# V computed once for each tile of 128 tokens and copied into its blocks; K's last four heads of chunks 2 and 3 computed in the padding of seven weight tiles; transfers issued from two queues

## The chip, the cores and the metric

The kernel runs on one core of a Trainium2 chip. The core has five engines, each with an instruction queue of its own that is worked off in order: TensorE (PE, matrix products into PSUM), VectorE (DVE), ScalarE (ACT), GpSimd (POOL) and SyncE (SP), which here only issues transfers (DMAs). Transfers can be issued by SP and by ACT; on ACT such an issue stands in the same queue as its arithmetic. The metric is the device time of one launch in microseconds (us); before the change the median of three runs is 171.44 us.

## What is computed

Inputs and output are bf16; 2048 tokens of width D = 448; 16 heads of Dh = 28; F = 1792. Cut to what matters:

```python
mod = silu(c) @ w_mod                      # six vectors: sa, ca, ga, sb, cb, gb
h = layernorm(x) * (1 + ca) + sa
q, k, v = split(h @ wqkv)                  # (16 heads, 2048, 28) each
idx = pos[:, None] - 2 * arange(8)         # each token sees itself and 7 earlier ones, 2 apart
logits = einsum(q, k[idx]) * 28 ** -0.5    # masked where idx < 0
o = einsum(softmax(logits), v[idx])
x = x + ga * (o @ wo)
h = layernorm(x) * (1 + cb) + sb
out = x + gb * (silu(h @ w1) @ w2)
```

## The kernel before

**Tokens.** Since a token sees only tokens of its own parity, the sequence is held as two parities of 1024 positions. It is worked in four chunks (`NC = 4`) of `CP = 256` positions of both parities, that is, 512 tokens. Attention works in nine blocks (`BLOCKS`, 0 to 8): block b has 112 queries of each parity (128 in block 0) and the 128 keys from position 112·b on, so neighbouring blocks share 16 keys.

**Stages of a chunk.** `norm1` normalises the 512 tokens and brings them, modulated, with the features on the partitions, into a buffer `h` (`h1_0`, `h1_1`, `wqk` in turn). For chunk 0 this is done in two halves with transposes on PE (L529) and the modulation on ACT and DVE (L536, L538); for the others by transposing DMAs on SP (L550) and a modulation in place (L555, L557). `project` computes Q and K by tiles of four heads, each head padded from 28 to 32 columns (weights `wp`, `wp3`, filled by four copies `pad`, L564 and L566): a "duo" is one tile of Q and the same tile of K, 14 matmuls (L627) of 64 contracted rows each, in pairs that run side by side, first seven "straight" then, after a `turn`, the "crossed" rest; a turn is an empty instruction of POOL (L312) that the crossed matmuls wait for. There are four duos a chunk (eight of half the width in chunk 0). The result is evicted to `qk` (L630). V is computed for each block (L638, 14 matmuls of 448 columns) and evicted into one of four buffers `v` (L642). Since a block's keys start up to 128 positions ahead of the chunk, `h` is 384 wide and a copy `halo` (L611) brings the end of the chunk before.

**Attention and the rest.** `logits` (L670) and the exponential (ACT, L678) run for each block and parity, DVE masks (L704), `values` multiplies with V (L730), DVE normalises (L735, L736), a transposing DMA (L740) brings the result to `oT`, `out_proj` (L753) and DVE (L768) add it to `x_all`. Then a second layernorm (`n2`), the first feed-forward product (L791, evicted with silu by ACT, L794), the second (L808; L832 for the last 256 tokens), the addition (L823, L838) and the store (L826, L841). `gate` (L450) and `mods` (L433) compute the modulation vectors from `w_mod`.

**What sets the order.** Every step is an operation of a `Plan`; the string `ORDER` lists all operations by number, and each engine's queue gets its steps in that order (a letter a or v puts a step on ACT or DVE). Buffers are handed out in the same order: four PSUM tiles `ps`, five `p`, four `v`. All DMAs share eight semaphores: a queue issues the ninth DMA only when an earlier one on the same semaphore has landed, and it holds everything behind it in that queue until then. Before the change nearly all DMAs are SP's; ACT issues three at the start (L368: the second half of chunk 0's `x` and the vector c).

The function is called twice: a second, `safe` version of the layer stands behind a flag worked out from the softmax sums and is skipped here.

Of the kernel before, what the change touches and what calls it, by code (L numbers as in the profile page):

```python
# [35 lines left out]
HW = 128 + CP  # L36
# [40 lines left out]
def half(j):  # L77
    return slice(K3 * j, K3 * j + K3)
# [33 lines left out]
def dram(ap, row, col, dims):  # L112

    w = ap.ap[0][0]
    return bass.AP(ap.tensor, ap.offset + row * w + col, [[r * w + c, n] for r, c, n in dims])


class Plan:

# [879 lines left out]
```

## Time and profile before

| what | value |
|---|---|
| median of three runs (lowest, highest) | 171.44 us (171.24, 171.64) |
| the profiled execution's own time | 171.64 us |
| its span, first to last instruction | 169.9 us |
| busy: PE, ACT, DVE, POOL | 162.0, 114.5, 96.1, 33.2 us |
| mean granted clock of PE | 0.989 |
| matmuls of V (L638), of Q and K (L627) | 126 and 280 |

The span and the time outside it (1.74 us) make the execution's own time. The profile has these views: busy time by engine; the chain of waits, followed back from the last instruction and shown in order of time (start, duration, what); groups of instructions by line; a timeline; sums by windows of time; who waited for whom; the transfers, with their time from issue to landing. A row of the timeline holds the start, the time that the row's instructions cover, the engine, line and operation, the tiles, the number of instructions (x14), and in brackets the engine's idle time before it with what ended it.

### The profile page before, as it was taken

How to read it: one execution, taken by the hardware profiler on the slowest of the kernel's cores; microseconds unless marked ns; L12 is line 12 of the kernel's file. 1: busy time of each engine (PE TensorE's matmuls, PEld its weight loads, DVE VectorE, ACT ScalarE, POOL GpSimd, SP SyncE). 2: the span in 40 equal slices, each digit the busy share in tenths (PEclk: the TensorE clock that was granted, in tenths of full speed). 3: DMA queues.
4: the chain of work that ended last, by engine and by line, in shares of the span. 5: the costliest groups of instructions: out<-in, count | busy, mean ns of one | idle time of the engine just before them, and what ended most of it. 6: DMA issues, size and time to landing. Idle time of an engine off the chain costs nothing.

```text
span 169.9 us, 4812 instructions
## 1 busy us (share of the span) xinstructions
PE 162.0 (95%) x2015; PEld 83.9 (49%) x2015; DVE 96.1 (57%) x189; ACT 114.5 (67%) x163; POOL 33.2 (20%) x88
## 2 busy tenths in 40 slices
PE   7799999899999999999999999999999999999990
PEld 2258644545554564455644544655544444445450
DVE  4777999899979963895352577732473000000451
ACT  3148999999876889999878998662767862420000
POOL 7342424730502221132000205120150000000000
PEclk9959999999999999999999999999999999999999
DMA  4994448489979874022020030086008000000031
GB/s 142 289 326 165 99 94 314 78 202 242 176 185 252 177 198 106 0 66 46 20 54 0 4 90 22 2 112 178 6 10 224 0 4 0 0 4 0 38 136 64
DMA packets 32054, 17.51 MB, mean 103 GB/s; under 512 B 23896, under 2 KB 31640, under 8 KB 32024
## 3 DMA queue, kind: packets, MB, share of 16 engines
q1 hardware_dynamic: 31872, 16.90, 39.9%
q8 instruction: 17, 0.28, 0.7%
q10 hardware_dynamic: 152, 0.23, 0.5%
q14 instruction: 13, 0.11, 0.2%
HBM read 9.12 MB, written 1.84 MB: 64 GB/s over the span
## 4 chain that ended last, share of the span: by engine, by line
PE 75%; ACT 10%; DMA 6%; issue 3%; DVE 2%; POOL 1%; ACTq 0%; POOLq 0%
PE ps L791 25%; PE ps L808 22%; PE ps L627 7%; PE ps L753 6%; PE ps L638 5%; ACT p L678 4%; PE ps L730 4%; DMA wqk<-in_A_wqkv_dram 3%; PE ps L832 3%; PE ps L670 3%; DMA x_all<-in_A_x_dram 2%; ACT h L536 2%; ACT qk L630 1%; POOL rs L487 1%; ACT both L480 1%
## 5 line engine op out<-in xcount | busy, mean ns | idle before, releaser
L791 PE MATMUL ps<-h,w 64*128 64x512 bf16 x392 | 44.7, 376 | 0.0
L808 PE MATMUL ps<-w,both 64*128 64x448 bf16 x392 | 39.9, 349 | 0.0
L794 ACT ACTIVATE both<-ps 128x1024 bf16<-128x1024 f32 x28 | 27.3, 1023 | 13.9 <-PE ps L791 13.8
L678 ACT ACTIVATE p<-ps 128x896 bf16<-128x896 f32 (+1 forms) x36 | 31.5, 928 | 3.3 <-PE ps L670 3.2
L791 PEld LDWEIGHTS <-w 64*128 64x128 bf16 x392 | 19.5, 94 | 21.6
L808 PEld LDWEIGHTS <-both 64*128 64x128 bf16 x392 | 18.9, 94 | 17.7
L823 DVE TENSOR_TENSOR ot<-ps,x_all 128x896 bf16<-128x896 f32 x7 | 7.6, 1088 | 34.6 <-PE ps L808 34.3
L627 PE MATMUL ps<-h,wp 64*128 64x256 bf16 (+1 forms) x224 | 20.4, 323 | 0.6 <-ACT h L536 0.4
L627 PEld LDWEIGHTS <-wp 64*128 64x128 bf16 x280 | 13.9, 94 | 11.3 <-issue 1.1
L704 DVE TENSOR_TENSOR p<-p,maskb 128x1792 bf16<-128x1792 bf16 (+1 forms) x18 | 19.3, 1098 | 0.0
L768 DVE SCALAR_TENSOR_TENSOR x_all<-ps,x_all 128x448 bf16<-128x448 f32 x16 | 9.3, 618 | 9.7 <-PE ps L753 9.7
L487 POOL TENSOR_TENSOR rs<-rs,negh 128x2 f32<-128x2 f32 x16 | 13.8, 861 | 1.3
L753 PE MATMUL ps<-wo,oT 64*128 64x448 bf16 x112 | 13.0, 350 | 0.0
L480 ACT ACTIVATE wqk<-x_all,mv 128x448 bf16<-128x448 bf16 x16 | 10.7, 667 | 3.2 <-POOL mv L477 3.0
L477 POOL TENSOR_SCALAR mv<-sums 128x2 f32<-128x2 f32 x10 | 4.8, 479 | 40.0 <-DVE x_all L768 22.2
L638 PE MATMUL ps<-wv,h 64*128 64x448 bf16 x98 | 11.3, 350 | 0.2
L557 DVE TENSOR_SCALAR h<-h,modc 128x512 bf16<-128x512 bf16 x19 | 6.8, 408 | 6.6 <-DMA h<-xn 6.6
L630 ACT CAST qk<-ps 128x1024 bf16<-128x1024 f32 (+1 forms) x12 | 10.0, 871 | 0.7 <-PE ps L627 0.7
L321 ACT ACT_TABLE_LOAD x8 | 10.3, 1283 | 0.1
L486 POOL TENSOR_SCALAR rs<-mv 128x2 f32<-128x2 f32 x10 | 3.6, 356 | 33.3 <-ACT wqk L480 14.5
L736 DVE TENSOR_TENSOR o<-ps,rc 112x896 bf16<-112x896 f32 (+1 forms) x9 | 9.8, 1091 | 0.4
L501 DVE TENSOR_SCALAR xn<-x_all,mv,rs 128x512 bf16<-128x512 bf16 x23 | 8.8, 406 | 1.7 <-POOL rs L487 1.7
(84 smaller groups left out, 161.8 us busy)
## 6 DMA issues: line engine op xcount, KB each, us to landing
out_dram<-ot SPq DMA_DIRECT2D x7, 224.0 KB, 2.2
both<-in_w_mod_dram SPq DMA_DIRECT2D x2, 672.0 KB, 6.0
x_all<-in_A_x_dram SPq DMA_DIRECT2D x3, 448.0 KB, 7.0
w<-in_B_w_dram SPq DMA_DIRECT2D x3, 448.0 KB, 4.2
w<-in_B_w_dram SPq DMA_DIRECT2D x1, 896.0 KB, 5.3
both<-in_w_mod_dram SPq DMA_DIRECT2D x2, 336.0 KB, 5.8
w<-in_B_w_dram SPq DMA_DIRECT2D x1, 672.0 KB, 5.4
wqk<-in_A_wqkv_dram SPq DMA_DIRECT2D x1, 448.0 KB, 5.7
```

The source lines that it names most:

```text
L321: P.load = lambda t: S.preload_act_table(ACTF.Exp if t == "e" else ACTF.Silu)
L480: S.activation(out=scratch[late], in_=x_all[:, us[j], :], func=ACTF.Square, bias=mv[:, j, 0:1], accum_out=mv[:, j, 1:2])
L487: G.tensor_tensor(out=rs[:, j:j + n], in0=rs[:, j:j + n], in1=negh[:, 0:n], op=ALU.pow)
L627: return T.matmul(ps[:, j, 0:2 * n], lhsT=w.rearrange("p h d -> p (h d)"), rhs=h[rows, :, t, c0:c0 + n], start=start, stop=stop)
L630: copy_on(o)(out=qk[:, :, g, :, s0:s0 + n], in_=ps[:, :, 0:2 * n].rearrange("p j (t s) -> p j t s", t=2))
L638: return T.matmul(ps[:, j, 0:D], lhsT=h[rows, j, t, b0:b0 + 128], rhs=wv[rows, t, :], start=start, stop=stop)
L678: S.activation(out=out_, in_=ps[:, :, 0:4 * nq].rearrange("p j (g q) -> p j g q", q=nq), func=ACTF.Exp, scale=SCALE)
L704: V.tensor_tensor(out=p, in0=p, in1=maskb[:, 1 if b == 0 else 0, 0:nq].unsqueeze(1).to_broadcast([128, H, nq]), op=ALU.mult)
L753: return T.matmul(box["ps"][:, j, 0:D], lhsT=oT[rows, j, kk, s0:s0 + 128], rhs=wo[rows, j, kk, :], start=start, stop=stop)
L791: return T.matmul(ps[:, j, :], lhsT=w, rhs=h[rows, :, t, :], start=start, stop=stop)
L794: S.activation(out=hid[:, k % 2, :, i, :], in_=ps[:], func=ACTF.Silu)
L808: return T.matmul(box["ps"][:, par, 0:D], lhsT=hid[rows, k % 2, f % 2, f // 2, 128 * (2 * i + par):128 * (2 * i + par) + 128], rhs=w2[rows ...
```

## The change

**V in tiles.** V is computed for eight tiles of 128 positions instead of nine blocks, each once, and evicted into three new buffers `va`. Blocks 0 and 8 read their tile directly. Each of the other seven blocks is put together from two neighbouring tiles by two transfers within SBUF (`vs`, 14 in all, 16 to 112 rows of 2048 bytes) into one of three buffers `v`. The `halo` copies go, and `h` is 256 wide.

**Q and K in seven tiles.** In chunks 2 and 3 K's last four heads (4 × 28 = 112 columns) are put into the padding columns of the seven other weight tiles (7 × 4 heads × 4 columns), by nine small copies on POOL (`fill`), two of which go into an extra weight tile `wq3`. The fourth duo then has a Q tile alone, with half the columns for each matmul (256 instead of 512). Four transfers a chunk (`mv`, 28 KB each) bring K's last heads from the padding rows to their place in `qk`. The projections of chunk 1 and later wait for the fills.

**Transfers.** A load, a `vs`, a `mv` or a store may stand on SP's queue or ACT's; `ORDER` says which. ACT now issues two loads of `w_mod` first, and 20 DMAs in all; the second half of chunk 0's `x` comes behind the weights of Q and K. Two pairs of loads of 64 rows (for `wqk3` and `w13`) become one load each, whose source is two pieces of 64 rows (`pairs_of`); a third load of this kind, of 28 KB, is new. `ORDER` is another string throughout, with another order of projections, of first-layer products and of table loads (6 in place of 8 behind the first).

```diff
-    NV, NP, NX, NO, NH, NB2 = (4, 5, 2, 2, 3, 2) if not safe else (3, 3, 2, 1, 3, 1)
+    NA, NV, NP, NX, NO, NH, NB2 = (3, 3, 5, 2, 2, 3, 2) if not safe else (3, 3, 3, 2, 1, 3, 1)
...
+def pairs_of(ap, r0, c0, r1, c1, n):
+
+    w = ap.ap[0][0]
+    return bass.AP(ap.tensor, ap.offset + r0 * w + c0, [[(r1 - r0) * w + c1 - c0, 2], [w, 64], [1, n]])
...
+    EITHER = ("sp", "act") if not safe else ("sp",)
+
+    def queue(o):
+        return nc.scalar if o["eng"] == "act" else nc.sync
...
-    ld_x = [[load(224, **first_x(0), run=1792, name="x0a"), load(224, **first_x(1), run=1792, q=nc.scalar, name="x0b")]]
+    ld_x = [[load(224, **first_x(0), run=1792, q=("sp",), name="x0a")]]
...
-    ld_ma = load_mod(0, 2 * D, [first])
+    ld_ma = load_mod(0, 2 * D, [], ("act",))
...
-    ld_qk = [[a], [b], [a], [load(56, wqk3[half(a), 0:D], A_wqkv[128 * (a + 1):128 * (a + 1) + K3, D * (1 - a):D * (2 - a)], late, name="wqk") for a in range(2)]]
+    ld_qk = [[a], [b], [a], [load(112, wqk3[:], pairs_of(A_wqkv, 128, D, 256, 0, D), late, name="wqk")]]
...
+    ld_x[0].append(load(224, after=[x["deps"][0] for x in [ld_qk[0][0], ld_qk[1][0], ld_qk[3][0]]], **first_x(1), run=1792, name="x0b"))
...
+    def fill(out_, m0, in_, t0, t1, deps, name="fill"):
+
+        to = out_[:, m0:m0 + 4 * (t1 - t0), DH:32].rearrange("p (t r) c -> p t r c", r=4)
+        return P.op(("pool", 300.0), lambda o: G.tensor_copy(out=to, in_=spread(in_, t0, t1)), deps, name=name)
...
-        halo[k] = P.op(either(60.0 + 0.83 * 8 * w, 60.0 + 0.26 * 8 * w), lambda o: copy_on(o)(out=h[:, :, :, 128 - w:128].rearrange("p t k s -> p (t k) s"),
...
+    def move(r, s0, n, deps):
+
+        return sp(680.0, lambda o: queue(o).dma_start(out=qk[32 * r:32 * r + DH, 1, 3, :, s0:s0 + n], in_=qk_t[32 * r + DH:32 * r + 32, 0:7, :, s0:s0 + n]), list(deps), 1700.0,
+                  kb=28.0, run=512, eng=EITHER, name="mv")[0]
...
-            for g in range(4):
+            for g in range(4 if k < 2 else 3):
...
+            if k > 1:
+
+                def make(ps, j, kk, rows, t, start, stop, c0=c0):
+                    w = wq3[rows, kk // 3] if j and kk in (1, 3) else wp[rows, kk, 12:16, :] if kk < 3 else wp3[rows, 12:16, :]
+                    return T.matmul(ps[:, j, 0:n], lhsT=w.rearrange("p h d -> p (h d)"), rhs=h[rows, :, t, c0 + n // 2 * j:c0 + n // 2 * j + n // 2], start=start, stop=stop)
...
+                done = done + [move(r, s0, n, done) for r in range(4)]
...
+        for t in (2 * k, 2 * k + 1):
+            def make(ps, j, kk, rows, kt, start, stop, t=t):
+                return T.matmul(ps[:, j, 0:D], lhsT=h[rows, j, kt, 128 * (t % 2):128 * (t % 2) + 128], rhs=wv[rows, kt, :], start=start, stop=stop)
...
+            def shifted(o, b, up):
+                r = 16 * b
+                to, way = (slice(r, 128), slice(0, 128 - r)) if up else (slice(0, r), slice(128 - r, 128))
+                queue(o).dma_start(out=v_of[b]()[to], in_=va_of[b - 1 + int(up)][way])
```

Three places show how `ORDER` moves instructions. The listings give an engine's instructions in the order of its queue; lines are those of the file that each listing is of, and a tile's number tells its buffers apart.

ACT from the table load to the first exponential, before. L418 and L420 are silu of c and its transpose `scT`, L564 a pad, L536 the modulation of chunk 0, L630 the evictions of Q and K, L321 the load of the exponential's table, L678 the exponential:

```order
L382 ACT_TABLE_LOAD
L418 ACTIVATE both<-both 4x128
L420 CAST scT<-ps_67 128x4
L564 COPY wp<-wqk 128x32x28
L536 ACTIVATE h_0_83<-ps_68,modc 128x2x128 x2
L536 ACTIVATE h_0_83<-ps_67,modc 128x2x128 x4
L630 CAST qk<-ps_69 128x2x2x128
L630 CAST qk<-ps_68 128x2x2x128
L630 CAST qk<-ps_66 128x2x2x128
L321 ACT_TABLE_LOAD
L678 ACTIVATE p_93<-ps_67 128x1024
```

The same stretch of ACT's queue in the changed kernel, from the transpose of c on (L556 is the modulation, L676 the eviction, L332 the table load, L383 a load):

```order
L440 CAST scT<-ps_67 128x4
L597 COPY wp_76<-wqk_74 128x16x28
L556 ACTIVATE h_0_84<-ps_69,modc 128x2x128 x2
L383 DMA both<-in_A_wqkv_dram 128x1x112
L383 DMA x_all<-in_A_x_dram 128x2x896
L383 DMA wv<-in_A_wqkv_dram 128x2x448
L383 DMA both<-in_w_mod_dram 128x3x448
L383 DMA both<-in_w_mod_dram 64x448
L676 CAST qk<-ps_68 128x2x2x128
L676 CAST qk<-ps_67 128x2x2x128
L676 CAST qk<-ps_66 128x2x2x128
L676 CAST qk<-ps_69 128x2x2x128
```

Five loads now stand between the modulation of the first half of chunk 0 and the first evictions; behind the last row come the modulation of the second half, the table load and the first exponential.

DVE in the changed kernel, from the first modulation of chunk 0 to the second (L558). L595 is a pad, L490 and L491 the statistics of 128 tokens, L521 the normalisation:

```order
L558 TENSOR_SCALAR h1_0_84<-ps3_69,modc_108 128x2x128 x2
L595 COPY wp_75<-wqk_72 128x32x28
L490 BN_STATS st_261<-x_all_70 128x6
L491 BN_AGGR mv_144<-st_261 128x2
L490 BN_STATS st_264<-x_all_70 128x6
L491 BN_AGGR mv_144<-st_264 128x2
L490 BN_STATS st_288<-x_all_70 128x6
L491 BN_AGGR mv_147<-st_288 128x2
L490 BN_STATS st_291<-x_all_70 128x6
L491 BN_AGGR mv_147<-st_291 128x2
L521 TENSOR_SCALAR xn1_83<-x_all_70,mv_144,rs_145 128x512 x2
```

Before, the statistics of both halves of chunk 0 stood ahead of all pads and modulations. Now those of the second half (`mv_144`) stand behind them, and its normalisation stands behind two statistics of chunk 1 (`mv_147`). PE's queue has moved alike: it had the transposes of both halves ahead of the first projection; now the second half's stand behind all four projections of the first half, followed by the first logits and only then by the second half's projections.

SP in the changed kernel, between the transposes of chunk 1 and of chunk 2 (L383 loads, L716 the `vs` transfers, L570 the transposes of chunk 2 into `wqk`):

```order
L383 DMA wo<-in_A_wo_dram 64x448
L383 DMA w_80<-in_B_w_dram 128x1x896
L383 DMA both<-in_w_mod_dram 64x448
L383 DMA x_all<-in_A_x_dram 128x2x896
L383 DMA both<-in_w_mod_dram 64x896
L383 DMA both<-in_w_mod_dram 128x3x896
L716 DMA v_93<-va_90 16x1024
L716 DMA v_93<-va_91 112x1024
L570 DMA_TRANSPOSE wqk<-xn_83 128x8x128
L716 DMA v_94<-va_91 32x1024
L570 DMA_TRANSPOSE wqk<-xn_83 128x8x128
```

Before, this stretch held six loads and then the two transposes with nothing between them. The load of chunk 3's `x` has come here from the start, and three `vs` transfers stand before or between the transposes.

More of the change, by code (lines that the diff above doesn't have):

```diff
@@ L35 @@
 BLOCKS = ((0, 1), (2, 3), (4, 5), (6, 7, 8))
-HW = 128 + CP
 WARM, JUNK = 8, 5
@@ L398, in layer @@
     ld_1.append(load(448, w1[:, 1, :].rearrange("p (a n) -> p a n", a=2), dram(B_w1, 128, 0, ((1, 0, 128), (64, F // 2, 2), (0, 1, F // 2))), late, run=1792, name="w1"))
-    ld_1 += [load(112, w13[half(a), :], B_w1[128 * (a + 1):128 * (a + 1) + K3, F // 2 * (1 - a):F // 2 * (2 - a)], late, run=1792, name="w1") for a in range(2)]
+    ld_1.append(load(224, w13[:], pairs_of(B_w1, 128, F // 2, 256, 0, F // 2), late, run=1792, name="w1"))
     ld_2 = [load(112.0 * (f1 - f0), w2[:, f0:f1, :], B_w2[128 * f0:128 * f1, :].rearrange("(f p) d -> p f d", p=128), late, name="w2") for f0, f1 in ((0, 8), (8, NF))]
@@ L596, in norm1 @@
         h = h1[k % NH]
-        after = [x for kk in (k - NH,) if kk >= 0 for x in qk_mm[kk] + v_mm[kk] + [halo[kk + 1]]] + (pads if k == 2 else [])
+        after = [x for kk in (k - NH,) if kk >= 0 for x in qk_mm[kk] + v_mm[kk]] + (pads + fills if k == 2 else [])
         if k == 0:
@@ L630, in ev @@
                     copy_on(o)(out=qk[:, :, g, :, s0:s0 + n], in_=ps[:, :, 0:2 * n].rearrange("p j (t s) -> p j t s", t=2))
-                m, e = duo(make, 2 * n, ready + pads, (either(act_ns(4 * n), dve_ns(4 * n)), ev, [], None), f"QK{k}.{i}.{g}")
+                m, e = duo(make, 2 * n, ready + pads + fills, (either(act_ns(4 * n), dve_ns(4 * n)), ev, [], None), f"QK{k}.{i}.{g}")
                 qk_mm[k] += m
                 done.append(e)
-            qk_done[k].append(done)
-        for b in BLOCKS[k]:
-            def make(ps, j, kk, rows, t, start, stop, b=b):
-                b0 = 128 + 112 * b - CP * k
-                return T.matmul(ps[:, j, 0:D], lhsT=h[rows, j, t, b0:b0 + 128], rhs=wv[rows, t, :], start=start, stop=stop)
-            def vev(o, ps, b=b):
-                v_of[b] = vb[v_take[b]["slot"]["v"]]
-                copy_on(o)(out=v_of[b][:, :, :, 0:DH], in_=ps[:, :, 0:D].rearrange("p j (h d) -> p j h d", d=DH))
-            ready = parts[0] if b == 0 else [x for p in parts for x in p]
-            m, e = duo(make, D, ready + ([halo[k]] if k else []) + ld_v, (either(act_ns(2 * D), dve_ns(2 * D)), vev, [], None), f"V{b}")
-            v_mm[k] += m
-            v_done[b] = e
-            v_take[b] = m[0] if safe else e
-            v_take[b]["take"] += ("v",)
```

111 lines of the change are left out of this document (77 added, 34 removed), and 44 rows, old and new, of the table ORDER.

## The prediction

> **What bounds the kernel now.** I read the shares first, then the chain of waits, then PE's own waits.
>
> ```profile
> PE 162.0 (95%) x2015; PEld 83.9 (49%) x2015; DVE 96.1 (57%) x189; ACT 114.5 (67%) x163; POOL 33.2 (20%) x88
> PE 75%; ACT 10%; DMA 6%; issue 3%; DVE 2%; POOL 1%; ACTq 0%; POOLq 0%
> ```
>
> PE holds three quarters of the chain, but where it does not is what matters here. In the chain in order of time (start, duration, what) the first 34 us run through transfers, ACT and DVE, with PE in between; from 34.01 on it is PE nearly without a break, to 165.99.
>
> ```profile
> 0.79 4.17 DMA x_all<-in_A_x_dram
> 4.97 5.66 DMA wqk<-in_A_wqkv_dram
> 11.79 2.85 ACT h L536 x6
> 16.75 0.59 ACT L321
> 34.01 0.37 PE ps L670 x14
> ```
>
> So there are two stages: a start in which loads, ACT and DVE set the pace, and a long stage in which each matmul less is time less. Windows by time (PE, PEld, DVE, ACT, POOL busy, clock, DMA share, GB/s) show the same:
>
> ```profile
> 5.00:10.00 5.00, 3.64 (x48) 2.10 (x47) 4.15 (x13) 0.23 (x2) 2.74 (x7) 0.93 1.02 298
> 15.00:20.00 5.00, 4.85 (x95) 4.04 (x92) 3.80 (x10) 4.42 (x7) 2.82 (x8) 1.00 0.18 43
> 25.00:30.00 5.00, 5.00 (x62) 2.29 (x58) 4.97 (x8) 4.94 (x12) 2.01 (x4) 1.00 0.82 281
> 30.00:35.00 5.00, 4.49 (x99) 2.70 (x94) 4.33 (x8) 4.85 (x8) 2.79 (x5) 1.00 0.57 110
> 40.00:45.00 5.00, 5.00 (x88) 2.71 (x83) 4.84 (x10) 4.68 (x7) 1.60 (x2) 1.00 1.12 183
> 120.00:140.00 20.00, 20.00 (x194) 9.33 (x190) 5.67 (x14) 14.39 (x21) 2.50 (x7) 1.00 0.19 51
> ```
>
> From 15 to 35 us ACT is busy for 4.4 to 4.9 of 5 us: there a lost ACT microsecond is lost for good, although PE reads "busy" (its matmul ends are modelled). Behind 120 us nothing but PE counts.
>
> **The change part by part.** *Matmuls removed* (term A). V loses one block of 14 matmuls, and the fourth duo of chunks 2 and 3 (14 each) goes from 512 to 256 columns. Prices are those of undisturbed rows of the chain, and of one timeline row for 256 columns:
>
> ```profile
> 71.76 0.76 PE ps L638 x8
> 45.92 1.73 PE ps L627 x16
> 14.69 2.91 PE L627 MATMUL ps<-h,wp 64*128 64x256 bf16 x50 [0.36 <-ACT h L536]
> ```
>
> 0.76/8 = 0.095 us, times 14 = 1.33. 1.73/16 = 0.108 against 2.91/50 = 0.058: 0.05 × 28 = 1.40. A = −2.7 us, all of it behind 34 us, where PE sets the end.
>
> *Tile changes on PE* (B). Matmuls of 64, 28 and 128 contracted rows alternate. Eight matmuls of the output projection take more right behind such a change:
>
> ```profile
> 42.20 0.86 PE ps L753 x8
> 49.41 0.76 PE ps L753 x8
> ```
>
> That is 0.10 for coming back; going over is not split out by the chain, and I take the same again as its upper bound. Counted in the two queues from the first projection on, the changed one has 53 changes, five more than before: 0.5 to 1.0 us, taken as 0.75.
>
> *The start* (D). The first projection needs the second piece of the Q/K weights. It was issued last of the four of the first row below (2.48 to 5.86, some 0.45 for one), at about 5.4; in the changed queue it stands on ACT and must wait for the landing of chunk 0's first x (4.96 in the chain), so again about 5.0 to 5.4. With a landing as in this view of the transfers (KB each, us to landing), it is there at 10.9 to 11.3, as now, and the first projection starts at about 12.5 (now 12.73).
>
> ```profile
> 2.48 3.38 SPq L368 DMA_DIRECT2D wqk<-in_A_wqkv_dram  x4
> ...
> wqk<-in_A_wqkv_dram SPq DMA_DIRECT2D x1, 224.0 KB, 5.9
> x_all<-in_A_x_dram SPq DMA_DIRECT2D x3, 448.0 KB, 7.0
> SPq L368 <- DMA x_all<-in_A_x_dram: 1.3, 1, 1.3
> ```
>
> (The last row is a wait of SP's queue for an earlier landing, of the sort that now also stands on ACT.) What is later is the second half of chunk 0: its x is issued at about 5.4 instead of 0.79 and, at 7.0 us, lands at 12.4. Then DVE does four statistics, two normalisations, PE two transposes of 128 tokens, ACT two modulations, by these rows:
>
> ```profile
> 12.45 0.63 DVE L470 BATCH_NORM_STATS2 st<-x_all 128x6 f32<-128x448 bf16 x1 [0.46 <-DMA x_all<-in_A_x_dram]
> 13.11 0.18 DVE L471 BATCH_NORM_AGGREGATE mv<-st 128x2 f32<-128x6 f32 x1
> 7.75 0.38 DVE L501 TENSOR_SCALAR xn<-x_all,mv,rs 128x512 bf16<-128x512 bf16 x1
> 8.19 0.40 PE L529 MATMUL ps<-ident,xn 128*128 128x128 bf16 x4 [1.26 <-DVE xn L501]
> ```
>
> 4 × 0.8 = 3.2 to 15.6, two × 0.38 to 16.4, a transpose 0.4 behind the last to 16.8, two modulations at 2.85/6 = 0.48 to 17.8. Now the second half's projections start when the first half's 56 matmuls are through: 26 before 14.69 and 30 of the row above, 14.69 + 30 × 0.058 = 16.4. So 1.4 us later. ACT arrives at the same: its five loads behind the first modulation cost about 0.43, 0.37, 0.56, 0.59 and 0.59 = 2.5 us of its queue,
>
> ```profile
> 1.22 0.85 ACTq L368 DMA_DIRECT2D both<-in_c_dram  x2
> 8.42 0.37 SPq L368 DMA_DIRECT2D x_all<-in_A_x_dram  x1
> 6.94 0.56 SPq L368 DMA_DIRECT2D wv<-in_A_wqkv_dram  x1
> 25.02 0.59 SPq L368 DMA_DIRECT2D both<-in_w_mod_dram  x1
> 14.50 0.61 ACT L630 CAST qk<-ps 128x512 bf16<-128x512 f32 x1
> 18.05 1.02 ACT L678 ACTIVATE p<-ps 128x1024 bf16<-128x1024 f32 x1
> ```
>
> so from about 12.2 to 14.7; four evictions (0.55 to 0.61) to 17.0, two modulations to 17.9, the table load (1.28) to 19.2, against 18.05 for the first exponential now. Behind the loads wait exactly these evictions, and PE's PSUM tiles for them. D = +1.4; at the low end 0 (224 KB less go ahead of the weights, 0.75 us at some 300 GB/s, and the rest is filled), at the high end 2.8 (if the weights are as late again as x).
>
> *ACT between the first exponentials* (E). One of four modulations of chunk 1 now stands on ACT, ahead of the exponentials of block 1, and the first `gate` eviction beside it; the projections of chunk 1 wait for the first.
>
> ```profile
> L555 ACT ACTIVATE h<-h,modc 128x512 bf16<-128x512 bf16 x5 | 3.8, 806 | 4.4 <-DMA h<-xn 4.4
> L453 ACT CAST gbc<-ps 128x448 bf16<-128x448 f32 x2 | 1.1, 540 | 0.0
> ```
>
> E = +0.8 (0 to 1.35). In return the second `gate` comes from the full stage into the start:
>
> ```profile
> 61.80 0.78 PE ps L450 x4
> ```
>
> If it fits PE's holes there it saves 0.78, else nothing: −0.4.
>
> *Fills and turns* (G). The trace has no copy on POOL; the nearest rows are a strided fill of as many elements, 0.20 us, and two-element arithmetic, up to 0.86. Nine fills in its queue stand among the turns; behind a late turn wait the crossed matmuls.
>
> ```profile
> L354 POOL MEMSET v<- 128x128 bf16 x4 | 0.6, 204 | 0.0
> L487 POOL TENSOR_TENSOR rs<-rs,negh 128x2 f32<-128x2 f32 x16 | 13.8, 861 | 1.3
> PEld L638 <- POOLq L312: 1.1, 2, 0.6
> ```
>
> The last row says what a turn on the path costs: 1.1 us for two. G = +0.3 (0 to 1.1). No gain is possible here.
>
> *Moved transfers* (H). 14 `vs` (1.8 MB in all, by 112 or 128 rows of 2 KB a block) and 8 `mv` join queues that are fullest at this time (DMA share 1.12 at 40 to 45). The nearest row is a copy within SBUF:
>
> ```profile
> wo<-wo SPq DMA_DIRECT2D x1, 224.0 KB, 5.3
> ```
>
> Between the V tiles and the product of their block stand some 8 to 12 us of PE work (four duos of 1.5, a tile of 1.3 and more), so 5.3 us are covered; if the cover is gone, the AV product is late by the difference. Five of these and other loads stand on ACT between 45 and 65 us, 2.5 us of a queue that is 85 to 95% full. H = +0.5 (0 to 3). The halo copies, nine normalisations moved from ACT to DVE and two table loads less lie beside PE: nothing, at best −0.6 where the chain passes a table load at 67.6.
>
> Sum: −2.7 + 0.75 + 1.4 + 0.8 − 0.4 + 0.3 + 0.5 = +0.65. On the profiled execution's own 171.64 (span 169.9 and 1.74 around it) that is 172.3; it stands 0.2 above the median of the runs, so against 171.44 I forecast 172.1.
>
> **The rivals.** *Faster* (0.36): the late second half is covered, since PE has its 3.2 us of first-half projections and the order was changed around just this; then D and E fall to 0 and A, B, half a gate remain, −2.35, or 169.1; with its own spread 168.3 to 170.8. For it: from 34 us on A is safe. Against it: ACT's rows above.
>
> *Few DMA engines* (0.16). The page's line on ACT's DMA queue
>
> ```profile
> q10 hardware_dynamic: 152, 0.23, 0.5%
> ```
>
> is 128 rows of x, 3 + 1 rows of c, and 20 packets more: 16 + 3 + 1, one for each engine that a load ran on, so the load of three rows ran on three of the 16. If a source in two pieces of 64 rows runs on two, `wqk3` (112 KB) puts 56 KB on each; at 298 GB/s over 16, 18.6 KB/us, that is 3.0 us instead of 0.4, and the second Q/K piece and x stand behind it in ACT's queue on those two. About half of the 2.6 is hidden, since SP's queue has 0.4 to 0.8 us of work there for each load anyway: D + 1.3, 173.4. The Trainium skill, "DMA: Bandwidth & Descriptors", in the section on why a DMA increments its semaphore by 16, says that a queue takes the largest number up to 16 that divides the slowest dimension of both sides, which for 128 and 2 would be two. By that rule the time is 173.4, without it 172.1; the count of 20 agrees with it for 3 and 1, and no run here yet shows 128 against 2.
>
> *Moved V or K lands late* (0.10): H at its upper end, from the point where a `vs` waits in SP's queue behind 1.9 MB of loads (6 us at 300 GB/s) and the 5.3 of its own, together over the cover: 174.2.
>
> *Same* is no mechanism but the case where D and E just eat A; it lies in the forecast's low edge.
>
> **How the numbers follow.** Forecast (later start, own range 171.5 to 173.0) 0.38; rivals 0.36, 0.16, 0.10. A difference under 0.2% (0.34 us) can't be told from none. Faster 0.36 from the first rival, with 0.01 of the forecast; same 0.09 from the forecast's low edge; slower the other 0.54. For 8 in 10 the range cuts a tenth on each side, into the first rival and the last: 168.7 to 174.1.
>
> **What would show it.** Right: in the chain, the second half's projections start 1 to 2.5 us later than 16.4 with ACT or DVE ahead of them, ACT's first exponential near 19.2, L638's successor at 112 matmuls, and behind 45 us PE without new waits. Wrong on D: first exponential at or before 18. Few engines: `wqk3` landing 2 us or more behind the first Q/K weights, DMAs with two closing packets. Wrong on H: PE waiting for a DMA into v or qk.

## The result and the profile after

The changed kernel takes 178.94 us (median of four runs, 177.47 to 181.1), against 171.47 for the kernel before: a ratio of 1.0408 (95% interval 1.0339 to 1.0477). The forecast was 172.1 with a range of 168.7 to 174.1. The sign was right; the loss is eleven times the +0.65 us of the sum. Ratios here leave out executions more than 1.5% above the fastest of their kernel, which for some of the last kernels below is half of them or more, so a ratio just under 1 there is not a kernel that is faster in every execution.

The shares of the changed kernel (engine, busy us, share of the span, instructions), and the chain by engine:

```profile
PE 159.6 (90%) x2001; PEld 82.3 (47%) x2001; DVE 96.0 (54%) x193; ACT 107.1 (61%) x153; POOL 31.6 (18%) x96
PE 62%; DMA 20%; DVE 10%; SPq 2%; POOL 2%; issue 1%; ACT 1%; DVEq 0%; POOLq 0%; ACTq 0%
```

PE does 2.4 us less (162.0 before), as it should, and the span is 6.9 us longer (169.9 to 176.8). PE's share of the chain fell from 75% to 62%; transfers rose from 6% to 20% and DVE from 2% to 10%. So the time went into waits. The same chain in order of time (start, duration, what) says where:

```profile
4.79 7.63 DMA x_all<-in_A_x_dram
12.45 0.64 DVE st L490
18.04 0.56 ACT h L556
18.65 2.12 PE ps L673 x18
22.31 0.62 DVE xn L521 x2
23.95 0.25 SPq L570
26.86 8.82 DMA x_all<-in_A_x_dram
35.70 0.64 DVE st L490
37.19 4.50 DMA wqk<-xn
52.43 4.78 DMA h<-xn
70.53 5.70 DMA oT<-o
```

Read downwards it is one late thing after another. The second half of chunk 0 is late (first rows). Chunk 1's second normalisation is then late on DVE (22.31), and SP, which holds its transpose in front of seven loads, issues them only from 24 us on. Chunk 3's x, the fifth of these, takes 8.82 us to land; its statistics stand on DVE ahead of chunk 2's second normalisation, so chunk 2's second transpose comes at 37.19 (32.6 before). The last three rows are transposes that take 4.5 to 5.7 us to land; behind 75 us, where little else is under way, one takes 2.6 to 2.8 in most cases.

The longer waits of PE in the timeline of the changed kernel, and a short one at 15.83 that matters below (the bracket holds the idle time ahead of the row and what ended it):

```profile
15.83 0.72 PE L549 MATMUL ps<-ident,xn 128*128 128x128 bf16 x8 [0.27 <-DVE xn L521]
18.20 4.68 PE L673 MATMUL ps<-h,wp 64*128 64x256 bf16 x48 [1.31 <-ACT h L556]
28.48 0.87 PE L673 MATMUL ps<-h,wp 64*128 64x512 bf16 x6 [0.69 <-ACT h L575]
54.14 0.93 PE L831 MATMUL ps<-wo,oT 64*128 64x448 bf16 x8 [0.74 <-DMA oT<-o]
58.79 0.94 PE L453 MATMUL ps<-scT,both 128*128 128x1 bf16 x32 [0.93 <-DVE x_all L846]
76.28 0.93 PE L831 MATMUL ps<-wo,oT 64*128 64x448 bf16 x8 [0.77 <-DMA oT<-o]
```

The events below are read from the timelines of the profiled executions of the two kernels and of four experiments (us; the starts of the first matmuls of each stage, the end of the last matmul, the span).

| | before | changed | e1 | e9 | e8 | e14 |
|---|---|---|---|---|---|---|
| first projection | 12.73 | 11.99 | 12.90 | 14.15 | 12.59 | 11.63 |
| second half's projections | 16.32 | 18.20 | 18.46 | 17.55 | 15.99 | 16.12 |
| first exponential | 18.05 | 19.91 | 20.18 | 19.27 | 17.72 | 17.84 |
| chunk 1's projections | 24.22 | 28.48 | 27.09 | 26.42 | 24.86 | 24.99 |
| chunk 2's projections | 37.68 | 42.82 | 41.88 | 40.25 | 38.70 | 37.96 |
| last matmul ends | 165.97 | 170.82 | 169.62 | 171.14 | 167.24 | 163.81 |
| span | 169.9 | 176.8 | 174.4 | 175.3 | 171.8 | 168.3 |

At chunk 2 the changed kernel is 5.1 us late, at the last matmul 4.85. What it saves behind 43 us, the holes at 54, 58 and 76 us (2.4 us together) take back. Another 2.1 us lie behind the last matmul (5.98 against 3.93): the last 112 KB store, issued at 171.51, still has packets under way at 174.5, beside fetches of instructions of 8 and 16 KB that hold single DMA engines for up to 1.6 us. In the experiments this end takes 4.0 to 5.4 us; no run was made on it.

### The profile page after: what moved, and what is told of

The parts are those of the page before. It is cut to its first block, busy times and chain, and to the rows that moved or that the text cites. A ratio compares the mean times of both kernels' runs of the same rounds, so it can differ in the third digit from the quotient of the medians.

```text
span 176.8 us, 4822 instructions
## 1 busy us (share of the span) xinstructions
PE 159.6 (90%) x2001; PEld 82.3 (47%) x2001; DVE 96.0 (54%) x193; ACT 107.1 (61%) x153; POOL 31.6 (18%) x96
## 4 chain that ended last, share of the span: by engine, by line
PE 62%; DMA 20%; DVE 10%; SPq 2%; POOL 2%; issue 1%; ACT 1%; DVEq 0%; POOLq 0%; ACTq 0%
PE ps L869 21%; PE ps L886 21%; DMA x_all<-in_A_x_dram 9%; PE ps L673 5%; PE ps L831 4%; DMA oT<-o 3%; PE ps L910 3%; PE ps L806 3%; DMA h<-xn 3%; DMA wqk<-xn 3%; DVE st L490 2%; PE ps L746 2%; DMA both<-in_c_dram 2%; SPq L383 2%; DVE xn L521 1%
## 5 line engine op out<-in xcount | busy, mean ns | idle before, releaser
L872 ACT ACTIVATE both<-ps 128x1024 bf16<-128x1024 f32 x28 | 27.5, 1021 | 14.8 <-PE ps L869 14.8
L869 PEld LDWEIGHTS <-w 64*128 64x128 bf16 x392 | 19.0, 94 | 22.2
L886 PEld LDWEIGHTS <-both 64*128 64x128 bf16 x392 | 18.4, 94 | 18.2 <-ACT both L872 0.7
L673 PE MATMUL ps<-h,wp 64*128 64x256 bf16 (+1 forms) x210 | 21.0, 338 | 3.3 <-ACT h L556 2.6
L673 PEld LDWEIGHTS <-wp 64*128 64x128 bf16 x252 | 13.1, 99 | 12.3 <-issue 5.1
L521 DVE TENSOR_SCALAR xn<-x_all,mv,rs 128x512 bf16<-128x512 bf16 x32 | 11.7, 407 | 7.3 <-POOL rs L507 7.3
L497 POOL TENSOR_SCALAR mv<-sums 128x2 f32<-128x2 f32 x10 | 3.4, 345 | 57.8 <-DVE x_all L846 27.0
L507 POOL TENSOR_TENSOR rs<-rs,negh 128x2 f32<-128x2 f32 x16 | 12.5, 780 | 1.3
L676 ACT CAST qk<-ps 128x1024 bf16<-128x1024 f32 (+1 forms) x12 | 9.8, 835 | 2.7 <-PE ps L673 2.6
L695 PE MATMUL ps<-wv,h 64*128 64x448 bf16 x84 | 10.0, 351 | 0.0
L806 PEld LDWEIGHTS <-p 128*128 128x128 bf16 x288 | 7.9, 96 | 3.3 <-issue 3.0
L831 PEld LDWEIGHTS <-oT 64*128 64x128 bf16 x112 | 5.2, 94 | 7.1 <-DMA oT<-o 2.4
```

The lines of the kernel that those rows point to most:

```text
L507: G.tensor_tensor(out=rs[:, j:j + n], in0=rs[:, j:j + n], in1=negh[:, 0:n], op=ALU.pow)
L521: V.tensor_scalar(out=out_, in0=in_, scalar1=mv[:, j, 0:1], scalar2=rs[:, j:j + 1], op0=ALU.subtract if b else ALU.add, op1=ALU.mult)
L673: return T.matmul(ps[:, j, 0:2 * n], lhsT=w.rearrange("p h d -> p (h d)"), rhs=h[rows, :, t, c0:c0 + n], start=start, stop=stop)
L695: return T.matmul(ps[:, j, 0:D], lhsT=h[rows, j, kt, 128 * (t % 2):128 * (t % 2) + 128], rhs=wv[rows, kt, :], start=start, stop=stop)
L806: T.matmul(box["ps"][:, par, h, 0:DH + 1], lhsT=p[:, at:at + 128], rhs=v[:, h, 0:DH + 1], start=True, stop=True)
L831: return T.matmul(box["ps"][:, j, 0:D], lhsT=oT[rows, j, kk, s0:s0 + 128], rhs=wo[rows, j, kk, :], start=start, stop=stop)
```

## The experiments

**Loads of two pieces, e1 to e4.** e1 issues the three loads of two pieces as two loads of 64 rows each.

```diff
-    ... load(112, wqk3[:], pairs_of(A_wqkv, 128, D, 256, 0, D), late, name="wqk")
+    ... load_two(112, wqk3[:], A_wqkv, 128, D, 256, 0, D, late, name="wqk")
...
+    def load_two(kb, out, src, r0, c0, r1, c1, n, after=(), run=896, name="ld"):
+        def go(o):
+            for i, (r, c) in enumerate(((r0, c0), (r1, c1))):
+                queue(o).dma_start(out=out[64 * i:64 * i + 64], in_=src[r:r + 64, c:c + n])
```

> The changed kernel, with the three loads whose source is two pieces of 64 rows (112, 28 and 224 KB) issued as two loads of 64 rows each; nothing else is changed. Theory 'few engines' (such a load runs on 2 of 16 DMA engines, and what stands behind it on those two is late): the second half of chunk 0's x lands before 11 us (12.42 in the changed kernel), the first exponential starts before 19 (19.91), chunk 3's x, landing at 35.67 there, lands at least 2 us earlier; 171.0 to 174.5 us. Theory 'late by its place' (x is late because it stands behind four loads on ACT's queue, whatever their shape): x lands within 0.5 of 12.4, first exponential 19.5 or later; 177 to 179.5 us.

e2 does this for the two loads of the start alone, e3 for the 224 KB load of `w13` alone.

> The changed kernel with only the loads of the start (112 and 28 KB) as two loads of 64 rows; the 224 KB load at 25 us stays one. Few engines: start as in the first run (x before 11, first exponential before 19), but chunk 3's x still takes over 7 us to land; between the two, 173.5 to 177 us. Late by its place: 177 to 179.5 us.

> The changed kernel with only the 224 KB load at 25 us as two loads of 64 rows. Few engines: the start unchanged (first exponential 19.9 within 0.3), chunk 3's x lands within 6.5 us of its issue (8.8); 174.5 to 177.5 us. Late by its place: the wait for chunk 3's x is only that of its late issue at 26.9, it takes 7 us or more as before; 177 to 179.5 us.

e4 does the reverse in the kernel before: its two loads of 56 KB become one load with two pieces.

```diff
-    ... [load(56, wqk3[half(a), 0:D], A_wqkv[128 * (a + 1):128 * (a + 1) + K3, D * (1 - a):D * (2 - a)], late, name="wqk") for a in range(2)]
+    ... [load(112, wqk3[:], pairs_of(A_wqkv, 128, D, 256, 0, D), late, name="wqk")]
```

> The kernel before, with its two 56 KB loads of wqk3 as one load whose source is two pieces of 64 rows; nothing else is changed. Few engines: this load, or what stands behind it on two engines, lands 2 us or more later than the 8.75 of before, the second piece of the Q/K weights (11.3) later by 1 us or more; 171.9 to 173.5 us. Late by its place: nothing moves by over 0.5 us, 171.1 to 171.8 us.

e1 took 176.06 us, ratio 1.0205 (1.0106 to 1.0304). e2 took 179.85 (175.94 to 182.25) and e3 178.78 (175.99 to 179.14), too wide for a ratio. e4 took 173.6 against 171.6, ratio 1.0135 (1.007 to 1.0201). So the shape of the loads costs time, in either kernel. But two of the expectations missed. In e1 and e2 the start did not get earlier: first exponential at 20.18 in both. (The granted clock is at half from 9.42 to 12.83 us in e1's trace and at full speed until 18.20 in the changed kernel's, so a few tenths between these two starts mean nothing.) And in e4 the second Q/K piece landed at 11.04, not later; it was the 448 KB piece that took 7.3 us instead of 5.7, and the first projection began at 13.26. That the load runs on few engines can be seen in the packets of ACT's queue, here those of 896 bytes (128 of `wqk3`, 256 of the second Q/K piece) counted by half microseconds from 6.0 us on:

```
start us   6.0 6.5 7.0  7.5  8.0 8.5 9.0 9.5 10.0 10.5 11.0
changed      9  18  54  140   53  31  24  22   11   12   10
e1          32  30   3  133  130  41  15   0    0    0    0
```

A packet takes 45 ns on average, so one engine would work off some 11 in half a microsecond. The changed kernel ends in a tail at the rate of two engines, then at half of it, 2 us longer than e1; from 9 us on 2.2 of these packets are under way at a time on average, from 10 us on 1.1, and never more than three. By the Trainium skill, "DMA: Bandwidth & Descriptors", section on why a DMA increments its semaphore by 16, the number of engines is the largest up to 16 that divides the slowest dimension of both sides, so a source whose slowest dimension is 2 gets two; the tail agrees. (Which engine a packet ran on isn't in the trace.)

Where the traces show a wait for such a load is behind that of `w13`. The first statistics of chunk 3 on DVE, in e2 (one load) and e3 (two loads):

```profile
35.18 0.63 DVE L496 BATCH_NORM_STATS2 st<-x_all 128x6 f32<-128x448 bf16 x1 [2.21 <-DMA x_all<-in_A_x_dram]
```

```profile
33.71 0.63 DVE L496 BATCH_NORM_STATS2 st<-x_all 128x6 f32<-128x448 bf16 x1
```

In e2 DVE waits 2.21 us for x, which was issued at 27.02, 8.2 us earlier; in e3, issued at 28.93, it is there within 4.8 us and nothing waits. The changed kernel has 8.82, e1 at most 4.6 (28.30 to 32.89). What each load costs in the end isn't shown: e2 and e3 are too scattered for that.

**The start, e5 to e9.** e5 puts the second half of chunk 0's x first on ACT, and its statistics and normalisation ahead of the pads (numbers in `ORDER` are operations: 25 the load, 89 to 92 statistics, 93 and 94 the normalisations).

```diff
-    "0 1 4 5 ... 14 25a 26 68 ... 81 82v ... 72 83v 73 ... 77a 89 90 ... 91 ... 92 107a 93v 94v ..."
+    "0 1 25a 26 4 5 ... 14 68 ... 81 89 90 91 92 82v ... 72 83v 93v 94v 73 ... 77a ... 107a ..."
```

> The run e1 (loads of 64 rows) with the start in the order of before: the second half of chunk 0's x is ACT's first issue, and its statistics and normalisation stand on DVE ahead of the pads and of the first modulation. Theory 'late start' (term D: the second half's statistics, behind the pads on DVE, set when chunk 0's second half, the first exponential and all behind them begin): the second half's projections start at 16.3 to 17.0 instead of 18.46, the first exponential at 18.0 to 18.8 instead of 20.18, and 1.0 to 2.5 us come off the 176.0 of e1: 173.5 to 175.2. Rival 'waits in the middle' (the time is set behind 30 us, by chunk 3's x and what waits behind it on DVE's and SP's queues): the start moves as said, but the end does not, 175.2 to 177 us.

e6 loads chunk 3's x (31) early, e7 does both.

```diff
-    "... 21 22 33a 34 ... 206 31 32 207a ..."
+    "... 21 22 31 32 33a 34 ... 206 207a ..."
```

> The run e1 with chunk 3's x loaded behind the weights of V on SP, as before the change, instead of behind five loads at 28 us. Late start: chunk 3's statistics on DVE come at 31 instead of 32.9, and chunk 2's second transposes at most 0.8 us earlier than 34.61; time within 0.7 of e1's 176.0. Waits in the middle: the first projection of chunk 2 starts at least 1 us earlier than 41.88, and 1 to 2.5 us come off, 173.5 to 175 us.

> Both of the last two. If the two causes add, 171.5 to 173.5 us, and the kernel is still not clearly faster than before, since the fills, the moved V and K and the lost cover between 40 and 60 us remain; if one theory holds alone, the time of its own run. If the forecast's rival (late start only, A gained behind it) were the whole of it, 169 to 170.5 us.

All three missed: 179.11, 177.38 and 176.68 us, ratios 1.0393 (1.0336 to 1.045), 1.0321 (1.0269 to 1.0373) and 1.0242 (1.0186 to 1.0299). The second half got no earlier. In e5 the second half was normalised at 9 to 10 us, and its projections began at 19.09 all the same. PE's timeline of e5 shows why:

```profile
12.64 4.34 PE L679 MATMUL ps<-h,wp 64*128 64x256 bf16 x56
16.92 0.62 PE L555 MATMUL ps<-ident,xn 128*128 128x128 bf16 x8
19.09 0.28 PE L679 MATMUL ps<-h,wp 64*128 64x256 bf16 x2 [0.97 <-ACT h L562]
```

The second half's transposes (L555) stand behind all 56 matmuls of the first half on PE, and behind them follow DVE's and ACT's modulations, one after the other, which no matmul can cover. In the changed kernel these transposes waited 0.27 us for DVE's normalisation (15.83 above), so x's path and PE's order end there at nearly the same time: my place for the delay (x's landing, DVE's statistics) is one of two, and taking it away alone gains nothing, since the order on PE and ACT holds the second half as long. Something else is in these three traces: the granted clock is at half from 8.05 to 14.88 us in e5, from 10.22 to 17.05 in e6 and from 9.02 to 15.85 in e7, twice as long as in e1, so the 56 matmuls take 4.34 us in e5 instead of 3.42. In e6 chunk 3's x no longer waits, but the first projection comes only at 13.77: ACT's silu of c stands in its queue behind issues of loads and comes at 8.89 instead of 6.17 in e1. That an earlier load of chunk 3's x brings nothing by itself is thus not shown.

e8 therefore takes the whole start from the kernel before: each step up to the second logits and the first transposes of chunk 1, on all engines and queues, then the rest of the changed kernel's order. The loads of `wx` and of the first gate follow the weights of V on SP. These are many moves at once (the transposes' place, the queues of the loads, chunk 3's x); what each is worth is not split up. e9 is e8 with the loads of two pieces as single ones.

```diff
-    "0 1 4 5 6 7 61 2 3 8 9 10 11 12 15a 16 13a 14 25a 26 68 ... 84 85 76v 65 87v ... 104 108 109 112 ... 95 96 ... 98v 97a ..."
+    "61 62 63 0 1 8 9 79v 78v 25a 26 2a 3 4a 5 10a 80 89v 90v ... 85 13 14 74a 95 96 65 86v ... 87a 88 112 113 98a 97a 99 100 31 32 ..."
```

> The run e1 with the whole start (every step up to the second logits and the first transposes of chunk 1, on all engines and both queues) in the order of the kernel before: loads on SP, both halves of chunk 0 transposed and modulated ahead of the first projection, chunk 3's x loaded early; from there on the changed kernel's order. Late start (term D, its place corrected: what is late is the second half's transposes and modulation, which stand behind all first projections on PE and ACT): the second half's projections start at 16.2 to 16.9 (18.5 in e1), the first exponential at 17.9 to 18.6 (20.2), chunk 1's projections by 25.5 (27.1); 170 to 172.5 us. Waits in the middle: the start moves as said, but fills, turns and moved blocks between 24 and 60 us take it back; 173 to 175.5 us.

> The run e8, but with the three loads of two pieces as one load each, as in the changed kernel. Few engines: 0.8 to 2.5 us over e8 in the same rounds (the first projection 0.3 to 1 us later, and the 224 KB piece at 21 to 26 us takes over 7 us). If the shape of the loads only mattered together with the late start: within 0.6 us of e8.

e8: 172.78 us, ratio 1.0028 (0.999 to 1.0066). e9: 176.87, ratio 1.0275 (1.0216 to 1.0334). In e8 the events came as expected or earlier (15.99, 17.72, 24.86), the time a little above the expected range; in e9 the loads cost 4.1 us, more than the 0.8 to 2.5 expected. With the changed kernel and e1 this makes a square, in which the loads and the start (as a whole) each stand alone:

| ratio to before | start of the change | start of before |
|---|---|---|
| loads of two pieces | 1.0408 | 1.0275 (e9) |
| two loads of 64 rows | 1.0205 (e1) | 1.0028 (e8) |

The loads cost 2.0 to 2.5% of 171.5 us, 3.5 to 4.2 us; the start 1.3 to 1.8%, 2.3 to 3.0 us. By the intervals of the ratios each of these differences is uncertain by 0.7 to 1.2 points of the percentage. Both together account for the loss but for 0.28%, which e8's interval can't tell from nothing. In e9's trace the loads' price is seen at the start, where nearly all loads are on one queue (first projection at 14.15 instead of 12.59). A second loss is at 50 us (e18 below has such a hole there without these loads, so it is not theirs alone):

```profile
52.96 0.93 PE L831 MATMUL ps<-wo,oT 64*128 64x448 bf16 x8 [2.59 <-DMA oT<-o]
60.00:65.00 5.00, 5.00 (x66) 2.11 (x64) 2.54 (x5) 3.36 (x4) 1.07 (x3) 0.79 1.00 104
```

The second row is of the view by windows; behind POOL's busy time stands the granted clock, 0.79, here in a stage in which PE is busy throughout.

**Where the 2.7 us of saved matmuls (term A) stay, e10 to e18.** e8 is level with the kernel before, though its PE work is that of the changed kernel, 2.4 us less. Two groups of rows of e8, of POOL with DVE beside it, and of the chain at 66 us:

```profile
24.03 1.65 POOL L597 COPY wp<-wqk 64x48 bf16<-64x48 bf16 x2 [0.87 <-PE ps L701]
25.65 1.17 POOL L510 TENSOR_TENSOR rs<-mv,epsb 128x2 f32<-128x2 f32 x1
```

```profile
24.35 2.41 DVE L786 TENSOR_TENSOR p<-p,maskb 128x2048 bf16<-128x2048 bf16 x2
```

```profile
66.30 6.37 DMA oT<-o
72.71 0.93 PE ps L837 x8
```

Two fills and an addition of two elements take 2.8 us beside DVE's masks (0.25 and 0.2 each elsewhere), and chunk 1's turn stands behind them. By the Trainium skill, "SBUF — State Buffer", section "Who interferes with whom", a DVE instruction with two SBUF inputs contends with a GpSimd instruction that reads SBUF; the rows agree. And at 66 us a transpose shares the queues with the 896 KB load of w2, issued on ACT at 64.09 (67.49 in the changed kernel). In the kernel before SP issued it:

```profile
59.76 0.57 SPq L368 DMA_DIRECT2D w<-in_B_w_dram  x1
```

It had landed there at 65.10, about when oT's transpose was issued (64.92). (The expectation of e10 names 34 us for it; the load at 34 us is w2's other one, of 672 KB.) e10 moves the 896 KB load to 14 us, e11 moves three fills (186, 188, 191) ahead of a turn and the rstd (228) behind two, e12 does both.

```diff
-    "... 41 42 ... 57a 58 ..."
+    "... 41 42 57 58 ..."
```

```diff
-    "... 184 363 ... 377 186 137 191 188 179a ... 365 228 205 209 ..."
+    "... 184 186 191 188 363 ... 377 137 179a ... 365 205 209 228 ..."
```

> The run e8 with the 896 KB load of w2, which stands on ACT at 64 us there (at 34 on SP in the kernel before), moved to SP behind the loads of the start (about 14 us, where the queues are nearly empty). Theory 'moved transfers collide' (term H: the 1.98 us hole of PE at 70.7 is oT's transpose, 6.37 us to landing instead of 2.7, behind this load and the vs transfers): the transpose at 66 lands in under 4.5 us and the hole shrinks to under 0.8; 0.8 to 2 us off e8. Rival 'only masked': another wait (vs, mv, the exponential) holds the second layer at the same time, within 0.5 us of e8.

> The run e8 with POOL's last three fills ahead of the turn of V1, and the first rstd of chunk 2 behind the turns of chunk 1's first two projections. Theory 'fills behind a DVE mask' (term G: the hole of 1.04 us at 25.9 is two fills and an rstd that take 2.8 us beside DVE's masks, with a turn behind them): the hole shrinks to under 0.4 and the first projection of chunk 1 starts 0.4 to 1 us earlier than 24.86 or runs through; 0.3 to 1 us off e8. Rival: ACT and DVE hold the stretch 25 to 40 us anyway, within 0.3 us of e8.

> Both of the last two. If they add: 169.5 to 171.3 us, faster than the kernel before by 0.2% or more; if only one holds, its own time.

e10: 174.87, ratio 1.0156 (1.0102 to 1.021); e11: 172.86, 1.0016 (0.9975 to 1.0057); e12: 173.74, 1.0036 (0.9991 to 1.0082). In e11 the hole at 25.9 is gone and the last matmul ends 0.65 earlier than in e8, which the times can't tell from none. In e10 the transpose at 70 us lands in 3.0 us and no hole follows, as expected; but at 14 us the load meets chunk 1's transposes (5.1 us instead of 2.8), and a hole of 3.96 us opens at 49. The collision at 70 us is real. That the new place is worse rests on e10 alone: e12, with the same move, loses nothing against e11 (1.0036 and 1.0016), and e16 and e18 below have such a hole near 49 us without it.

e13 moves oT2's transpose (399) ahead of two vs transfers and a modulation of chunk 3 (312) behind two additions (404, 405). e14 puts w2's load on SP behind oT4's transpose (435), on e11. e15 does both.

```diff
-    "... 307 308 223 224 ... 399 400 ... 312v 403 404 405 406 ..."
+    "... 307 308 399 400 223 224 ... 403 404 405 312 406 ..."
```

```diff
-    "... 435 436 420 ... 421 57a 58 160 ..."
+    "... 435 436 57 58 420 ... 421 160 ..."
```

> The run e11 with two steps moved between 41 and 53 us: oT2's transpose ahead of two vs transfers and of the second transposes of chunk 3 on SP, and the last two additions to x_all (chunk 0) ahead of the first modulation of chunk 3 on DVE, which waits for a transpose. Theory 'queue order' (the holes of 1.56 us at 47.3 and 1.2 at 52.5 are steps that are ready and stand behind one that waits): together they shrink by 1.3 us or more; 0.8 to 2 us off e11, 170 to 171.2. Rival 'the next wait takes over' (the squares on ACT, POOL's rstd and the second transposes of chunk 3 hold the same stretch): the first hole shrinks, the end moves by less than 0.5.

> The run e11 with the 896 KB of w2 on SP directly behind oT4's transpose (65.4) instead of on ACT 2 us ahead of it. Collision (term H): oT4's transpose lands in under 4 us (6.6 in e11), the hole of 2.05 us at 70.0 shrinks to under 0.8, and nothing else is late, since w2 is not used before 78: 1 to 2 us off e11. Rival: mv and vs alone make the transpose late; within 0.4 of e11.

> Both of the last two. If both theories hold and add: 168.3 to 170.2 us, clearly faster than the kernel before (171.5), which is what terms A and B alone would give (169.1). If the waits only take each other's place: 171 us or more.

e13: 178.49, ratio 1.0365 (1.0303 to 1.0427); e15: 176.51, 1.0263 (1.0206 to 1.032). The edit had lost the letter of 312, and the modulation went over to ACT. There it waited for its transpose ahead of an eviction and of two mv transfers, as ACT's timeline of e13 shows:

```profile
53.74 0.81 ACT L581 ACTIVATE h<-h,modc 128x512 bf16<-128x512 bf16 x1 [7.15 <-DMA h<-xn]
54.46 0.56 ACT L693 CAST qk<-ps 128x512 bf16<-128x512 f32 x1
55.05 1.67 ACTq L654 DMA_DIRECT2D qk<-qk  x2
```

One waiting instruction of 0.81 us, put ahead of two transfers on ACT, costs 4.8 us (e15 against e14) to 6.0 (e13 against e11); in e13's trace the holes that it leaves in PE are followed by 6.83 us at half clock. It tells nothing about the queue order that it was meant for. e14: 172.18, ratio 0.9982 (0.9933 to 1.003). oT4's transpose lands in 2.63 us (6.61 in e11) and no hole follows, so the collision is settled in the trace, but not in the time. Its profiled execution, the fastest of twelve, shows what the change can do: span 168.3, last matmul at 163.81, 2.2 us earlier than before, and the chain runs through PE nearly without a break from 50 us on:

```profile
63.47 0.57 PE ps L837 x6
64.04 0.76 PE ps L701 x8
64.79 0.65 PE ps L875 x6
65.46 4.06 PE ps L875 x36
```

e16 and e17 repeat the two moves of e13 on e14, one after the other and with 312 left on DVE; e18 is e14 again.

> The run e14 with the first modulation of chunk 3 behind the last two additions to x_all on DVE, where it stays on DVE (in e13 it had gone over to ACT, ahead of an eviction and of two mv transfers, which its wait then held for 5 us). Queue order: the hole before the mods at 52 (0.55 in e14, 1.2 in e11) goes, 0 to 1 us off e14. Rival: nothing moves, within 0.4 us.

> The run e16 with oT2's transpose ahead of two vs transfers on SP. Queue order: the hole at 47.7 (0.77) goes too; 0 to 0.8 us off e16. Rival 'the next wait takes over': the vs transfers are then late for the fourth block's product, or the eight semaphores hold another transfer; 0 to 2 us over e16.

> The kernel of e14 once more, beside the last two on the same chip, to settle whether it is faster than the kernel before: 170.0 to 172.4 us, a ratio of 0.993 to 1.003 by its first runs.

e16: ratio 0.9926 (0.9884 to 0.9968), median over all its executions 173.08 (169.63 to 176.5). e17: 0.9952 (0.991 to 0.9994), median 171.33 (169.74 to 173.93). e18: 0.9885 (0.9838 to 0.9931), median 171.18 (169.45 to 175.17). The two moves do nothing that can be told from e14 and e18, which are one kernel and differ by as much. The kernel now has executions 1% faster than the median of the one before (169.45 to 169.63 us against 171.51), but not all, and the median over all its executions is not clearly below. The same program shows both. PE's row at 50 us and the window from 50 to 55 us, in e18:

```profile
50.47 0.99 PE L837 MATMUL ps<-wo,oT 64*128 64x448 bf16 x6 [2.99 <-DMA oT<-o]
50.00:55.00 5.00, 4.53 (x32) 2.28 (x33) 1.23 (x4) 1.47 (x3) 0.00 (x0) 0.66 0.79 201
```

and that window in e14:

```profile
50.00:55.00 5.00, 4.63 (x107) 3.02 (x102) 4.02 (x14) 3.88 (x10) 1.44 (x4) 1.00 0.75 221
```

In e18 oT2's transpose was issued at 45.96 behind chunk 3's (41.21, which took 3.36 us to issue) and landed 4.4 us later; PE stood for 2.99 us, and then the granted clock was half for 3.4 us: the 28 matmuls behind the hole (L837 and L701 in turn) take 4.5 us instead of 2.8. In e14 the issue of chunk 3's transpose took 1.87 us and the hole was 0.42. That issue stands three places behind w2's other load on SP, of 672 KB at 37 us, and ends within 0.1 us of that load's landing in both (43.63 in e14, 44.49 in e18); why it waits for it, and why the load lands later in e18, was not tried.

## Why the prediction was wrong

*What bounds the kernel* was right for the kernel before: a start set by loads, ACT and DVE, then PE. That PE goes on setting the pace behind 34 us in the changed kernel was not: the holes at 54, 58 and 76 us are DMA's and DVE's. Behind 123 us neither kernel has a wait of PE.

*Term A* (−2.7) holds roughly in PE's busy time (−2.4, with B's changes and other stretches at half clock in it), and the end of the last matmul in e14's fastest execution (−2.2) shows that it can reach the end when the waits are gone. B and the gate's −0.4 were not measured by themselves.

*Term D* (+1.4) was right in its events, half right in their cause and too small. The second half's projections came at 18.20 (forecast 17.8), the first exponential at 19.91 (19.2). x landed at 12.42 (forecast 12.4) by luck: it was issued 0.6 us earlier and was under way 0.6 us longer. But ACT's five loads cost nothing, since the evictions waited for PE behind them:

```profile
13.97 2.27 ACT L676 CAST qk<-ps 128x512 bf16<-128x512 f32 x4 [1.57 <-PE ps L673]
```

and an x and statistics in time did not help by themselves (e5), since the transposes stand behind the first projections as long. In size the start costs 2.3 to 3.0 us by the square. What the term left out, as the trace shows it, is what follows: SP's queue held by a transpose until 24 us, and 18 matmuls at half clock (2.12 us at 18.65, 0.118 each instead of 0.058).

*E* (+0.8) isn't shown. PE waits 0.69 us for chunk 1's modulation on ACT at 28.48, but that modulation had waited for its own transpose, issued at 22.95 instead of 19.41 before:

```profile
27.62 0.81 ACT L575 ACTIVATE h<-h,modc 128x512 bf16<-128x512 bf16 x1 [1.00 <-DMA h<-xn]
```

*G* (+0.3) is seen only where a DVE mask runs beside the fills (a hole of 0.69 us in e8, with the last matmul 0.65 earlier in e11); the times can't tell it from nothing. In the changed kernel itself the fills take 0.2 to 0.36 us each.

*The loads of two pieces* are the step that failed most: the sum has them at nothing, and they cost 3.5 to 4.2 us in all. They were in the rival "few DMA engines", whose rule fits the packets; its chance (0.16), its price (D + 1.3) and its place were wrong. I counted `wqk3` alone, and x behind it at the start, but the start did not get earlier when that load was split (e1, e2); only with nearly all loads on one queue (e4, e9) does it move the first projection. The front part names two pairs of loads that become one each, and the other, `w13` at 25 us, has twice the bytes and chunk 3's x behind it.

*H* (+0.5) had the wrong transfers: no matmul waited for a moved V or K. What the moved transfers do is to make transposes late (oT, 4.4 to 6.6 us to landing), above all w2's 896 KB, whose own move from 59.8 us on SP to 67.5 on ACT I didn't cost. The 10% rival named the cover of V and K and so a wait that never came; its 174.2 doesn't follow from H's upper end either, which makes the sum 3.15 and the time 174.6.

*The first rival (faster, 169.1)*: its claim, that the start would be covered, is refuted; its number is near what e14's kernel reaches in its best executions (169.45 to 170.1), which is luck, since that kernel has another start and other loads; it also leaves G and H out of its sum without a word (with them 169.9).

What stays open is the rest of term A: with loads and start mended, e8 is level with the kernel before and not 2.4 us faster. The traces show the holes (26, 48 to 54 and 70 us), but no run shows what each is worth.

## What to carry to other kernels

When one load replaces two, look at the slowest dimension of its source and at what is queued behind it, for each such load and not only for the first one. A step that is late at the start is priced by the queues that it holds (which loads stand behind its transpose, which normalisation behind its statistics), not by its own delay. Moving a large load is a change of its own: see which small transfer now shares the queues with it, and whether PE waits for that one.

## What the runs showed of the hardware

The granted clock fell to half in the middle of a busy stage. It changes in steps of 3.41 us, and a step at half clock followed a stretch of 3.41 us with 2.99 us of idle PE (e18), 2.5 (e16), 2.1 (e3) and 1.6 (the changed kernel, 14.8 to 18.2 us). Stretches with 1.74 and 1.71 us of idle PE (e5, from 76.3 and 52.4 us on) were not followed by one, so the idle time of one stretch alone doesn't decide near 1.7. Matmuls take about twice as long in such a step (0.118 us instead of 0.058), so one of 3.41 us costs up to 1.7 us on top of the hole. The Trainium skill, "TensorE: Matmul & The Clock Gate", sections "What's actually happening" and "HAM oscillation — how this bites in real kernels", gives a window of about 3.4 us and warns of idle gaps longer than that; here partly idle windows were enough. The trace of the kernel before has no such step between 13 and 166 us, and its 23 executions beside e16 spread over 1.3% (170.6 to 172.85). The 14 of e16 spread over 4%: in the six up to 171.15 us the mean granted clock is 0.982 to 1.0, in the eight from 172.74 us on 0.969 to 0.979 (one step at half clock takes 0.01 from the mean).
